# Dilated and plain sliding attention with a gated convolution: one score tile and one normalization per pair, constant matmuls at the start, evictions on ScalarE, plain v from DRAM, loads three groups ahead

## The chip, the cores and the metric

One core of a Trainium2 chip. The metric is the device time of one execution in microseconds (us). A run over 1.5% above the fastest of the same kernel counts as slow here; ratios use fast runs alone.

Engines: PE is TensorE (matmul and transpose), PEld its weight loads, DVE is VectorE, ACT is ScalarE, POOL is GpSimd, SP is the engine that issues most DMAs.

## The reference

```python
# q, k, v: (batch 8, heads 8, seq 576, dim 64)
scores = q @ k.T / sqrt(64)
mask_plain = (rel >= 0) & (rel < 32)                       # heads 0-3, rel = query - key
mask_dil   = (rel >= 0) & (rel < 128) & (rel % 4 == 0)     # heads 4-7
attn = softmax(where(mask, scores, -1e9));  x = attn @ v   # -> (8, 576, 512)
gate = sigmoid(causal depthwise conv of x, 5 taps)
out  = (gate * (x @ w_val)) @ w_out                        # fp32, (8, 576, 512)
```

The work is cut into 32 pairs of heads, four to a batch (two plain, two dilated). A pair is two halves: scores, exp, mask, product with v, normalization. Convolutions, value projections and output tiles of earlier pairs are put between these steps to keep PE busy. Two pairs of one kind in one batch form a group, which is the unit of loading.

## The kernel before

The order of instructions is written by hand and engines run their queues in order. The parts that matter:

```python
NET = 4
ets = [consts.tile([128, 2 * HB + 96], BF16, name=f"et{i}") for i in range(NET)]   # HB = 288
out_pool = tc.tile_pool(name="osb", bufs=4)
ps_sc = tc.tile_pool(name="ps_sc", bufs=2, space=PSUM)
...
def scores(i, hf):
    ps = ps_sc.tile([128, 2, 512], FP32, name="ps_sc")      # two banks, one for each head
    ...                                                     # 6 matmuls
    et = ets[(2 * i + hf) % NET]
    nc.scalar.activation(out=e3, in_=ps[:, :, 0:HB], func=AF.Exp, scale=scale)
...
def attn_v(i, hf):                                          # into the same tile, after the exp
    nc.tensor.matmul(out=ps[:, sl, n * AVS:n * AVS + D + 1], lhsT=et[...], rhs=rhs, ...)
def normalize(i, hf):                                       # reciprocal, then product, per half
...
for i in range(NP):
    if c % 2 == 0 and g + 2 < 2 * B:
        load_group(g + 2)
    ...                                  # casts of group g + 1, v casts, masks
    if i == 1:
        load_weights()                   # w_val and w_out, issued on POOL
    scores(i, 0); scores(i, 1)
    ...                                  # trans_x(i - 1)
    apply_mask(i, 0); pop_dense(0.5); pop_conv(i); apply_mask(i, 1)
    trans_main(g + 1, ...)               # transposes of the next group, evictions to ACT and DVE
    attn_v(i, 0); normalize(i, 0); pop_conv(i + 0.5)
    attn_v(i, 1); normalize(i, 1); pop_dense(1.5)
```

Names in the profile lines: `ps_sc` is the score tile in PSUM, `et` the exponentials, `xn` the normalized attention output, `xT` its transpose, `y_all` the gated value projections, `osb` an output tile in SBUF, `k_nat` and `k_b` the keys as loaded and as cast, and `qT`, `qA`, `kA`, `kB` the transposed queries and keys.

The softmax here doesn't subtract the row's maximum and nothing guards it: scores larger than these inputs give would overflow.

## Time and profile before

| | before |
|---|---|
| median of the runs, us | 208.59 (207.0 to 209.9) |
| start of pair 0, pair 4, pair 28, us | 11.36, 35.72, 167.19 |
| batches from pair 4 on, us | 21.79, 22.37, 22.57, 20.67, 22.50, 21.57 |
| busy: PE, DVE, ACT, POOL, us | 170.7, 136.3, 100.2, 51.6 |

A "batch" here is the time from the first score matmul of one pair to that of the fourth pair after it. The waits and busy times are in the prediction. The timeline of PE in the kernel before (start, length, line, operation; idle time before it in brackets), then that of ACT at the same place:

```profile
112.58 0.29 PE L357 MATMUL ps_sc<-qA,kA 64*128 64x128 bf16 x4
112.71 0.18 PE L357 MATMUL ps_sc<-qB,kB 64*128 64x32 bf16 x2
112.98 0.28 PE L357 MATMUL ps_sc<-qA,kA 64*128 64x128 bf16 x4
```

### The profile page before, as it was taken

How to read it: one execution, taken by the hardware profiler on the slowest of the kernel's cores; microseconds unless marked ns; L12 is line 12 of the kernel's file. 1: busy time of each engine (PE TensorE's matmuls, PEld its weight loads, DVE VectorE, ACT ScalarE, POOL GpSimd, SP SyncE). 2: the span in 40 equal slices, each digit the busy share in tenths (PEclk: the TensorE clock that was granted, in tenths of full speed). 3: DMA queues.
4: the chain of work that ended last, by engine and by line, in shares of the span. 5: the costliest groups of instructions: out<-in, count | busy, mean ns of one | idle time of the engine just before them, and what ended most of it. 6: DMA issues, size and time to landing. Idle time of an engine off the chain costs nothing.

```text
span 206.6 us, 5215 instructions
## 1 busy us (share of the span) xinstructions
PE 170.7 (83%) x2016; PEld 123.5 (60%) x2036; DVE 136.3 (66%) x370; ACT 100.2 (49%) x183; POOL 51.6 (25%) x99
## 2 busy tenths in 40 slices
PE   0277779879987999796979999779996998899990
PEld 0165556657655776565657766557675765675540
DVE  3357629589677966784679867758596856883510
ACT  2152442436644576354545755355743685354141
POOL 3063543026210450117011701062105303000000
PEclk9999999999999999999999999999999999999999
DMA  6968998399687985899489938995789766001435
GB/s 161 229 183 248 236 210 223 120 291 192 191 245 200 225 238 149 251 269 258 116 274 267 245 100 275 271 217 188 221 254 221 240 183 230 3 15 63 129 84 169
DMA packets 57186, 40.72 MB, mean 197 GB/s; under 512 B 25925, under 2 KB 52549, under 8 KB 57162
## 3 DMA queue, kind: packets, MB, share of 16 engines
q1 hardware_dynamic: 55280, 38.75, 72.6%
q0 software_dynamic: 1056, 1.05, 3.2%
q10 hardware_dynamic: 826, 0.60, 1.1%
q8 instruction: 16, 0.26, 0.6%
q14 instruction: 8, 0.07, 0.1%
HBM read 31.99 MB, written 9.44 MB: 201 GB/s over the span
## 4 chain that ended last, share of the span: by engine, by line
PE 39%; DMA 25%; DVE 14%; ACT 8%; SPq 6%; issue 4%; POOL 2%; ACTq 0%; POOLq 0%
DMA q_nat<-in_q_dram 22%; PE ps_moe L489 10%; PE ps_moe L459 10%; PE ps_moe L474 6%; DVE xn L408 5%; ACT et L360 3%; SPq L106 3%; PE ps_sc L389 3%; PE ps_sc L357 3%; PE ps_tr L286 3%; DMA vB_st<-in_v_dram 3%; ACT kA L307 2%; DVE y_all L480 2%; DVE et L373 2%; PE ps_tr L420 2%
## 5 line engine op out<-in xcount | busy, mean ns | idle before, releaser
L459 PE MATMUL ps_moe<-xT,conv_diag 128*128 128x288 bf16 (+1 forms) x384 | 53.1, 276 | 0.8 <-ACT osb L494 0.5
L360 ACT ACTIVATE et<-ps_sc 128x576 bf16<-128x576 f32 x64 | 38.6, 649 | 28.0 <-PE ps_sc L357 25.3
L474 PE MATMUL ps_moe<-xT,w_val_b 128*128 128x288 bf16 x256 | 39.9, 285 | 8.0 <-DVE y_all L480 7.3
L467 ACT ACTIVATE gate<-ps_moe 128x288 bf16<-128x288 f32 x64 | 26.7, 418 | 35.7 <-PE ps_moe L459 35.6
L459 PEld LDWEIGHTS <-conv_diag 128*128 128x128 bf16 x384 | 33.2, 101 | 8.7 <-issue 1.8
L408 DVE TENSOR_TENSOR xn<-ps_sc,rec 96x384 bf16<-96x384 f32 (+1 forms) x64 | 35.6, 555 | 2.2
L489 PE MATMUL ps_moe<-w_out_b,y_all 128*128 128x512 bf16 x124 | 33.9, 378 | 1.1
L480 DVE SCALAR_TENSOR_TENSOR y_all<-gate,ps_moe 128x288 bf16<-128x288 bf16 x64 | 27.6, 448 | 9.0 <-PE ps_moe L474 8.3
L474 PEld LDWEIGHTS <-w_val_b 128*128 128x128 bf16 x256 | 23.3, 97 | 17.1 <-issue 10.2
L494 ACT ACTIVATE osb<-ps_moe 128x512 f32<-128x512 f32 x36 | 21.5, 598 | 21.3 <-PE ps_moe L489 17.0
L435 DVE COPY xT<-ps_tr 128x576 bf16<-128x576 bf16 x32 | 14.6, 457 | 22.5 <-PE ps_tr L433 16.2
L171 POOL CAST vA<-v_st 128x512 bf16<-128x512 f32 x16 | 10.7, 671 | 56.0 <-DMA v_st<-in_v_dram 40.3
L389 PEld LDWEIGHTS <-et 128*128 128x128 bf16 x384 | 20.1, 102 | 6.0 <-DVE et L373 2.5
L489 PEld LDWEIGHTS <-y_all 128*128 128x128 bf16 x144 | 12.7, 97 | 11.8 <-issue 0.4
L403 DVE RECIPROCAL rec<-ps_sc 96x6 f32<-96x6 f32 (+1 forms) x64 | 11.9, 185 | 9.6 <-PE ps_sc L389 9.2
L373 DVE TENSOR_TENSOR et<-et,mask_p 128x576 bf16<-128x576 bf16 x32 | 15.2, 483 | 2.4 <-ACT et L360 1.9
L373 DVE TENSOR_TENSOR et<-et,mask_d 128x576 bf16<-128x576 bf16 x32 | 16.5, 532 | 0.2
L286 PE MATMUL ps_tr<-ident,k_b 128*128 128x128 bf16 x64 | 6.6, 242 | 11.2 <-POOL k_b L158 5.8
L168 POOL COPY vP<-vP 32x640 f32<-32x640 f32 x16 | 11.7, 752 | 16.6 <-DMA vP<-in_v_dram 13.9
L158 POOL CAST k_b<-k_nat 128x512 bf16<-128x512 f32 x14 | 9.0, 640 | 25.3 <-DMA k_nat<-in_k_dram 24.4
L301 ACT COPY kT<-ps_tr 128x1024 bf16<-128x1024 bf16 (+1 forms) x9 | 8.3, 917 | 13.0 <-PE ps_tr L286 12.9
L389 PE MATMUL ps_sc<-vP,et 128*128 128x65 bf16 x192 | 12.0, 200 | 2.3 <-DVE et L373 1.5
(66 smaller groups left out, 184.3 us busy)
## 6 DMA issues: line engine op xcount, KB each, us to landing
k_nat<-in_k_dram SPq DMA_DIRECT2D x15, 512.0 KB, 5.8
q_nat<-in_q_dram SPq DMA_DIRECT2D x15, 512.0 KB, 6.9
vP<-in_v_dram SPq DMA_DIRECT2D x8, 576.0 KB, 8.5
v_st<-in_v_dram SPq DMA_DIRECT2D x8, 512.0 KB, 4.2
vB_st<-in_v_dram SPq DMA_DIRECT2D x16, 128.0 KB, 5.0
out_dram<-osb SPq DMA_DIRECT2D x8, 256.0 KB, 3.5
out_dram<-osb SPq DMA_DIRECT2D x8, 224.0 KB, 3.1
out_dram<-osb SPq DMA_DIRECT2D x8, 192.0 KB, 3.4
```

Source lines behind the costliest of these rows:

```text
L286: nc.tensor.transpose(out=ps[:, z, TM * m:TM * m + TM], in_=src, identity=ident)
L360: nc.scalar.activation(out=e3, in_=ps[:, :, 0:HB], func=AF.Exp, scale=scale)
L373: nc.vector.tensor_tensor(out=e3, in0=e3, in1=m, op=ALU.mult)
L389: nc.tensor.matmul(out=ps[:, sl, n * AVS:n * AVS + D + 1], lhsT=et[:, sl * HB + col:sl * HB + col + 128], rhs=rhs, start=True, stop=True)
L408: nc.vector.tensor_tensor(out=dst, in0=av[:, :, :, 0:D], in1=rec[0:R, :, :, None].to_broadcast([R, 2, 3, D]), op=ALU.mult)
L435: nc.vector.tensor_copy(xTs[b % NXT][:, c, :, 2:], pr)
L459: nc.tensor.matmul(out=ps[:, o * T:(o + n) * T], lhsT=conv_diag[:, c, K - 1 - m, :], rhs=xt[:, c, r:r + n, off:off + T], start=(idx == 0), ...
L467: nc.scalar.activation(out=gate, in_=ps[:, 0:HB], func=AF.Tanh, scale=0.5)
L474: nc.tensor.matmul(out=ps[:, 0:HB], lhsT=w_val_b[:, mc, c * 128:(c + 1) * 128], rhs=xt[:, mc, 2 * G:2 * G + 2, 2:], start=(mc == 0), stop= ...
L480: nc.vector.scalar_tensor_tensor(out=y_all[:, c, b * S + G * HB:b * S + (G + 1) * HB], in0=gates.pop((b, c, G)), scalar=1.0, in1=ps[:, 0:H ...
L489: nc.tensor.matmul(out=ps, lhsT=y_all[:, c, 128 * n:128 * n + 128], rhs=w_out_b[:, c, :], start=(c == 0), stop=(c == NCH - 1),)
L494: nc.scalar.mul(out=osb, in_=ps, mul=0.5)
```

## The change

Its intent: warm PE early with matmuls on constants; halve the number of normalizations; take the 32 rows of overlap of plain v from DRAM instead of by POOL copies; move the qT, qA and kB evictions from DVE to ACT; give the loads one group more of a head start. Not in its short description, but in the diff: the next group's transposes move ahead of the masks, and the casts move two groups ahead, in front of the weight loads on POOL.

```diff
-    ps_sc = tc.tile_pool(name="ps_sc", bufs=2, space=PSUM)
+    ps_sc = tc.tile_pool(name="ps_sc", bufs=1, space=PSUM)
-    NET = 4
-    ets = [consts.tile([128, 2 * HB + 96], ...
+    NET = 2
+    ets = [consts.tile([128, 4 * HB + 96], ...
 ... (load of plain v as 128 overlapping rows; its POOL copies gone; masks rebuilt for the new layouts)
 def scores(i, hf):
-    ps = ps_sc.tile([128, 2, 512], FP32, name="ps_sc")
+    if hf == 0:
+        st[(i, "ps")] = ps_sc.tile([128, 4, 512], FP32, name="ps_sc")
+    ps = st[(i, "ps")][:, 2 * hf:2 * hf + 2, :]
 ...
 def attn_v(i, hf):
-    out=ps[:, sl, n * AVS:n * AVS + D + 1],
+    out=ps[:, 2 * hf, x * AVS:x * AVS + D + 1],
 ...
-def normalize(i, hf):      # reciprocal of 6, product of 384, per half
+def normalize(i):          # reciprocal of 12, product of 768, per pair
 ...
-    nc.vector.tensor_copy(t["qA"], ...)     # likewise qT, kB (kB in a new layout)
+    nc.scalar.copy(out=t["qA"], ...)
 ...
+    load_group(2)                            # at the start
+    warm(8)                                  # 128x512 matmuls on constants, 36 in all
 ... (in the loop over pairs)
-        load_group(g + 2)
+        load_group(g + 3)
 ... (casts of group g + 2 on POOL, ahead of load_weights)
         scores(i, 0)
         scores(i, 1)
+        trans_main(g + 1, ...)               # was behind apply_mask(i, 1)
         apply_mask(i, 0)
 ... (warm(2) or warm(3) at four places while i < 3)
         attn_v(i, 0)
-        normalize(i, 0)
         attn_v(i, 1)
-        normalize(i, 1)
+        normalize(i)
```

More of the change, by code (lines that the diff above doesn't have):

```diff
@@ L9 @@
 BF16 = mybir.dt.bfloat16
+I32 = mybir.dt.int32
 AF = mybir.ActivationFunctionType
@@ L68 @@
     ps_tr = ctx.enter_context(tc.tile_pool(name="ps_tr", bufs=2, space=PSUM))
-    ps_sc = ctx.enter_context(tc.tile_pool(name="ps_sc", bufs=2, space=PSUM))
+    ps_sc = ctx.enter_context(tc.tile_pool(name="ps_sc", bufs=1, space=PSUM))
     ps_moe = ctx.enter_context(tc.tile_pool(name="ps_moe", bufs=2, space=PSUM))
@@ L77 @@
     ident5 = consts.tile([8, 8], FP32, name="ident5")
-    mask_p = consts.tile([128, 4, 24], BF16, name="mask_p")
+    mask_p = consts.tile([128, NB, 96], BF16, name="mask_p")
+    junk = consts.tile([128, 512], BF16, name="junk")
+    same = consts.tile([128, 2], BF16, name="same")
+    par_i = consts.tile([128, 2], I32, name="par_i")
     mask_d = consts.tile([128, HB], BF16, name="mask_d")
@@ L81 @@
     kTs = [consts.tile([128, 2, KOFF + S], BF16, name=f"kT{i}") for i in range(NKT)]
-    NET = 4
-    ets = [consts.tile([128, 2 * HB + 96], BF16, name=f"et{i}") for i in range(NET)]
+    NET = 2
+    ets = [consts.tile([128, 4 * HB + 96], BF16, name=f"et{i}") for i in range(NET)]
     NVP = 2
@@ L130, in load_v @@
         if not dil:
+            dst = vPs[b % NVP].rearrange("p h n e -> p (h n) e")
+            first = 0
+            if b == 0:
+                nc.sync.dma_start(out=dst[32:128, 0, 0:D], in_=v[0, 0, 0:96, :])
+                first = 1
             nc.sync.dma_start(
-                out=vPs[b % NVP].rearrange("p h n e -> p (h n) e")[32:128, :, 0:D],
-                in_=v[b, 0:4].rearrange("h (t p) d -> p (h t) d", p=96))
+                out=dst[:, first:4 * NB, 0:D],
+                in_=bass.AP(
+                    tensor=v.tensor, offset=v.offset + (b * H * S + 96 * first - 32) * D,
+                    ap=[[D, 128], [96 * D, 4 * NB - first], [1, D]]))
         else:
@@ L139, in load_v @@
                 in_=v[b, 4:8, 0:RM, :].rearrange("h (p r) d -> p h (r d)", r=DIL))
-            for f in range(2):
-                nc.sync.dma_start(
-                    out=t["vBst"][64 * f:64 * f + 64].rearrange("p h j d -> p h (j d)"),
-                    in_=v[b, 4:8, DIL * TB:S, :].rearrange(
-                        "h (p f j) d -> f p h (j d)", f=2, j=2)[f])
+            nc.sync.dma_start(
+                out=t["vBst"].rearrange("p h j d -> p h (j d)"),
+                in_=v[b, 4:8, DIL * TB:S, :].rearrange("h (p j) d -> p h (j d)", j=2))
     def load_group(g):
@@ L165, in prep_v @@
         e = a + 2
-        if not dil:
-            vt = vPs[b % NVP]
-            nc.gpsimd.tensor_copy(
-                vt[0:32, a:e, 1:NB, 0:D], vt[96:128, a:e, 0:NB - 1, 0:D])
-        else:
+        if dil:
             nc.gpsimd.tensor_copy(
@@ L189 @@
     nc.scalar.dma_start(out=conv_nat, in_=moe_conv_w)
+    nc.vector.memset(junk, 1.0)
     nc.gpsimd.memset(ident, 0.0)
@@ L199 @@
     for et in ets:
-        nc.vector.memset(et[:, 2 * HB:], 1.0)
+        nc.vector.memset(et[:, 4 * HB:], 1.0)
     for i in range(NVP):
         nc.vector.memset(vPs[i][:, :, :, D:D + 1], 1.0 - 2.0 ** -9)
-        nc.vector.memset(vPs[i][0:32, :, 0, 0:D + 1], 0.0)
+        if i == 0:
+            nc.vector.memset(vPs[i][0:32, 0, 0, 0:D], 0.0)
     def band(dst, pattern, base):
@@ L222 @@
     )
-    band(mask_p, [[1, 4], [4, 24]], 32)
+    band(mask_p[:, 1, :].rearrange("p (r t) -> p r t", r=4), [[1, 4], [4, 24]], 32)
+    nc.gpsimd.tensor_copy(mask_p[:, 2:NB, :], mask_p[:, 1:2, :].to_broadcast([128, NB - 2, 96]))
+    nc.gpsimd.tensor_copy(mask_p[:, 0, :], mask_p[:, 1, :])
+    nc.gpsimd.memset(mask_p[0:32, 0, :], 0.0)
     for a in (0, 2):
@@ L248, in make_mask_d @@
         nc.gpsimd.tensor_copy(mask_d[:, TM:2 * TM], mask_d[:, 0:TM])
-        band(mask_d[:, 2 * TM:HB].rearrange("p (w t) -> p w t", w=2), [[64, 2], [1, TR]], TM - TB)
+        mb = mask_d[:, 2 * TM:HB].rearrange("p (w t) -> p w t", w=2)
+        nc.gpsimd.memset(mb, 1.0)
+        for (lo, up) in ((True, 0), (False, 0)):
+            sg = 1 if lo else -1
+            base = 2 * (TM - TB) if lo else 2 * (window - 1) - 2 * (TM - TB)
+            nc.gpsimd.affine_select(
+                out=mb, in_=mb, compare_op=ALU.is_ge, fill=0.0, base=base,
+                pattern=[[sg, 2], [2 * sg, TR]], channel_multiplier=-sg)
+        nc.gpsimd.iota(par_i, pattern=[[1, 2]], base=1, channel_multiplier=1)
+        nc.vector.tensor_scalar(
+            out=par_i, in0=par_i, scalar1=1, scalar2=None, op0=ALU.bitwise_and)
+        nc.vector.tensor_copy(same, par_i)
+        nc.vector.tensor_tensor(
+            out=mb, in0=mb, in1=same[:, :, None].to_broadcast([128, 2, TR]), op=ALU.mult)
     def setup_conv_w():
@@ L291, in trans_main @@
                     t["qT"] = qt_pool.tile([128, 2, DIL, T], BF16, name="qT")
-                nc.vector.tensor_copy(
-                    t["qT"][:, z0:z1, :, 0:TM],
-                    ps[:, z0:z1, :].rearrange("p z (r t) -> p z r t", r=DIL))
+                qd, qs = t["qT"][:, z0:z1, :, 0:TM], ps[:, z0:z1, :].rearrange("p z (r t) -> p z r t", r=DIL)
+                if g == 0:
+                    nc.vector.tensor_copy(qd, qs)
+                else:
+                    nc.scalar.copy(out=qd, in_=qs)
             else:
                 t["qA"] = qt_pool.tile([128, 2 * RM], BF16, name="qA")
-                nc.vector.tensor_copy(t["qA"], ps.rearrange("p z n -> p (z n)"))
+                nc.scalar.copy(out=t["qA"], in_=ps.rearrange("p z n -> p (z n)"))
         else:
@@ L305, in trans_main @@
                 t["kA"] = qt_pool.tile([128, 2 * RM], BF16, name="kA")
-                t["kB"] = qt_pool.tile([128, 8, 64], BF16, name="kB")
+                t["kB"] = qt_pool.tile([128, 4, 64, 2], BF16, name="kB")
                 nc.scalar.copy(out=t["kA"], in_=ps.rearrange("p z n -> p (z n)"))
-                nc.vector.tensor_copy(
-                    t["kB"][:, :, 0:TM - TB],
-                    ps.rearrange("p z (m t) -> p (z m) t", t=TM)[:, :, TB:TM])
+                nc.scalar.copy(
+                    out=t["kB"][:, :, 0:TM - TB, :],
+                    in_=ps.rearrange("p z (h w t) -> p (z h) t w", h=2, w=2)[:, :, TB:TM, :])
     def trans_rest(g):
@@ L327, in trans_rest @@
             nc.vector.tensor_copy(
-                t["kB"].rearrange("p (h w) t -> p h w t", w=2)[:, :, :, TM - TB:64],
-                pv[:, :, 0:64].rearrange("p w (h t) -> p h w t", h=4))
+                t["kB"][:, :, TM - TB:64, :],
+                pv[:, :, 0:64].rearrange("p w (h t) -> p h t w", h=4))
             nc.vector.tensor_copy(
@@ L352, in scores @@
                 else:
-                    x = 2 * (a + hf)
                     o = ps[:, sl, 2 * TM:HB]
-                    lhsT = t["kB"][p0:p0 + D, x:x + 2, :]
+                    lhsT = t["kB"][p0:p0 + D, a + hf, :, :]
                     rhs = t["qB"][p0:p0 + D, a + hf, :, :]
                 nc.tensor.matmul(out=o, lhsT=lhsT, rhs=rhs, start=True, stop=True)
-        et = ets[(2 * i + hf) % NET]
-        e3 = et[:, 0:2 * HB].rearrange("p (h n) -> p h n", h=2)
+        et = ets[i % NET]
+        e3 = et[:, 2 * hf * HB:2 * (hf + 1) * HB].rearrange("p (h n) -> p h n", h=2)
         nc.scalar.activation(out=e3, in_=ps[:, :, 0:HB], func=AF.Exp, scale=scale)
-        st[(i, "ps", hf)] = ps
-        st[(i, "et", hf)] = et
+        st[(i, "et")] = et
     def apply_mask(i, hf):
         b, c, dil, g, a = pair_info(i)
-        et = st[(i, "et", hf)]
-        if dil:
-            e3 = et[:, 0:2 * HB].rearrange("p (h n) -> p h n", h=2)
-            m = mask_d[:, None, :].to_broadcast([128, 2, HB])
-        else:
-            e3 = et[:, 0:2 * HB].rearrange("p (h n) -> p h n", h=6)
-            m = mask_p.rearrange("p r t -> p (r t)")[:, None, :].to_broadcast([128, 6, 96])
+        et = st[(i, "et")]
+        e3 = et[:, 2 * hf * HB:2 * (hf + 1) * HB].rearrange("p (h n) -> p h n", h=2)
+        m = mask_d if dil else mask_p[:, 3 * hf:3 * hf + 3, :].rearrange("p n q -> p (n q)")
+        m = m[:, None, :].to_broadcast([128, 2, HB])
         nc.vector.tensor_tensor(out=e3, in0=e3, in1=m, op=ALU.mult)
@@ L376, in attn_v @@
         b, c, dil, g, a = pair_info(i)
-        et, ps = st[(i, "et", hf)], st[(i, "ps", hf)]
+        et, ps = st[(i, "et")], st[(i, "ps")]
         for n in range(3):
@@ L388, in attn_v @@
                         rhs = vBs[b % NVD][:, a + hf, sl, 0:D + 1]
+                x = 3 * sl + n if dil else 2 * n + sl
                 nc.tensor.matmul(
-                    out=ps[:, sl, n * AVS:n * AVS + D + 1],
-                    lhsT=et[:, sl * HB + col:sl * HB + col + 128],
+                    out=ps[:, 2 * hf, x * AVS:x * AVS + D + 1],
+                    lhsT=et[:, (2 * hf + sl) * HB + col:(2 * hf + sl) * HB + col + 128],
                     rhs=rhs, start=True, stop=True)
-    def normalize(i, hf):
+    def normalize(i):
         b, c, dil, g, a = pair_info(i)
-        ps = st[(i, "ps", hf)]
         R = 128 if dil else 96
-        if hf == 0:
-            st[(i, "xn")] = xn_pool.tile([128, 2, 3, 2, D], BF16, name="xn")
-        xn = st[(i, "xn")]
-        av = ps[0:R, :, 0:3 * AVS].rearrange("p h (n e) -> p h n e", n=3)
-        rec = rec_pool.tile([128, 2, 3], FP32, name="rec")
+        xn = st[(i, "xn")] = xn_pool.tile([128, 2, 3, 2, D], BF16, name="xn")
+        av = st[(i, "ps")][0:R].rearrange("p (f s) c -> p f s c", f=2)[:, :, 0, 0:6 * AVS].rearrange(
+            "p f (x e) -> p f x e", x=6)
+        rec = rec_pool.tile([128, 2, 6], FP32, name="rec")
         nc.vector.reciprocal(out=rec[0:R], in_=av[:, :, :, D])
         if dil:
-            dst = xn[0:R, :, :, hf, :]
+            dst = xn[0:R].rearrange("p z n h d -> p h (z n) d")
         else:
-            dst = xn[0:R, hf, :, :, :].rearrange("p n h d -> p h n d")
+            dst = xn[0:R].rearrange("p z n h d -> p z (n h) d")
         nc.vector.tensor_tensor(
             out=dst, in0=av[:, :, :, 0:D],
-            in1=rec[0:R, :, :, None].to_broadcast([R, 2, 3, D]), op=ALU.mult)
+            in1=rec[0:R, :, :, None].to_broadcast([R, 2, 6, D]), op=ALU.mult)
     def trans_x(i):
@@ L546, in push_conv, with warm @@
             convs.append((t + 0.5 * G, ("c", b, c, G)))
+    def warm(n):
+        for _ in range(n):
+            ps = ps_moe.tile([128, 512], FP32, name="ps_moe")
+            nc.tensor.matmul(out=ps, lhsT=junk[:, 0:128], rhs=junk, start=True, stop=True)
+    warm(8)
     for z in range(2):
@@ L552 @@
             trans_rest(0)
+            warm(1)
+    setup_conv_w()
     for i in range(NP):
         b, c, dil, g, a = pair_info(i)
-        if c % 2 == 0 and g + 2 < 2 * B:
-            load_group(g + 2)
-        if a == 0 and g % 2 == 1 and g + 1 < 2 * B:
-            for z in (0, 2):
-                for name in ("k", "q"):
-                    cast(g + 1, name, z, nc.gpsimd)
+        if c % 2 == 0 and g + 3 < 2 * B:
+            load_group(g + 3)
         if i + 1 < NP:
@@ L565 @@
             make_perm()
+        g2 = g + 2
+        if g2 < 2 * B and g2 % 2 == 0:
+            cast(g2, "k" if a == 0 else "q", 0, nc.gpsimd)
+            cast(g2, "k" if a == 0 else "q", 2, nc.gpsimd)
         if i == 1:
@@ L569 @@
         scores(i, 1)
-        if i == 0:
-            setup_conv_w()
         if i > 0:
@@ L576 @@
                 queue_batch(b - 1)
-        if i < NCH:
-            make_conv_diag(i)
-        apply_mask(i, 0)
-        pop_dense(0.5)
-        pop_conv(i)
-        apply_mask(i, 1)
         if g + 1 < 2 * B:
@@ L588 @@
                 trans_rest(g + 1)
+        if i < NCH:
+            make_conv_diag(i)
+        apply_mask(i, 0)
+        if i < 3:
+            warm(2)
+        pop_dense(0.5)
+        pop_conv(i)
+        apply_mask(i, 1)
+        if i < 3:
+            warm(2)
         attn_v(i, 0)
-        normalize(i, 0)
         pop_conv(i + 0.5)
+        if i < 3:
+            warm(2)
         attn_v(i, 1)
-        normalize(i, 1)
+        normalize(i)
+        if i < 3:
+            warm(3)
         pop_dense(1.5)
```

## The prediction

> **What bounds the kernel now.** I read the engine totals first: TensorE (PE) busy 83%, VectorE (DVE) 66%, ScalarE (ACT) 49%, GpSimd (POOL) 25%. No engine is full on average, so the limit has to be found by stage. I took the start of each of the 32 pairs' score matmuls from the timeline of PE: pair 0 starts at 11.36 us, pair 4 (the second batch) at 35.72, pair 8 at 57.51, pair 28 at 167.19, and the end is 206.6. The busy times in just these stretches:
>
> ```profile
> 11.36:35.72 24.36, 18.98 (x185) 14.37 (x184) 16.15 (x37) 9.34 (x17) 12.41 (x24) 1.00 0.97 221
> ...
> 79.88:102.45 22.57, 19.53 (x251) 14.31 (x253) 15.84 (x43) 11.95 (x22) 5.65 (x10) 1.00 0.86 218
> 102.45:123.12 20.67, 19.31 (x251) 14.34 (x253) 16.53 (x43) 11.95 (x22) 6.10 (x10) 1.00 0.88 231
> 123.12:145.62 22.50, 19.47 (x250) 14.35 (x253) 15.74 (x43) 11.74 (x22) 5.75 (x10) 1.00 0.84 224
> ```
>
> The columns are length, then PE, weight loads, DVE, ACT and POOL busy. A batch in the steady state costs PE 19.3 to 19.5 us of 20.7 to 22.6: PE sets the pace and loses 1.4 us in the best batch and 3 in the others. What it loses them to is the list of PE's waits over the whole run:
>
> ```profile
> PE ps_moe L474 <- DVE y_all L480: 7.3, 7, 1.2
> PE ps_tr L286 <- POOL k_b L158: 5.8, 4, 1.7
> PE ps_tr L286 <- DVE k_b L158: 4.9, 1, 4.9
> PE ps_tr L317 <- DVE qT L292: 3.5, 1, 3.5
> PE ps_sc L357 <- DVE xn L408: 3.4, 9, 0.6
> ```
>
> The third and fourth belong to the first 10 us. The first comes once a batch: three value projections follow the last attention matmul, and the third waits for the `y_all` product that stands behind the normalization on DVE. The second is a DMA in disguise, since POOL's casts wait for loads:
>
> ```profile
> POOL k_b L158 <- DMA k_nat<-in_k_dram: 24.4, 6, 5.9
> POOL q_b L158 <- DMA q_nat<-in_q_dram: 9.1, 6, 1.8
> ```
>
> The chain of waits agrees: it spends 22% of the span in loads of q, at the start and again near 73, 86, 137 and 151 us. The first two batches are slow for another reason. The same convolution matmul, in the window from 34 to 36.5 us and in that from 36.5 to 45:
>
> ```profile
> L459 PE MATMUL ps_moe<-xT,conv_diag 128*128 128x288 bf16 x4 | 1.4, 443 | 0.0
> ```
>
> ```profile
> L459 PE MATMUL ps_moe<-xT,conv_diag 128*128 128x288 bf16 x9 | 1.9, 286 | 0.0
> ```
>
> A convolution of six matmuls takes 1.2 us from start to start before 36.5 us and 0.62 after it. PE runs at half its rate for the whole first batch and never again, although the granted clock reads 1.00 throughout.
>
> **What the Trainium skill says.** "TensorE: Matmul & The Clock Gate", Part 1, says that the array starts at half clock and that "activity releases the throttle", after about 3.4 us of sustained work, and that it falls back after an idle window. The trace agrees on the factor (443 against 286 ns), but not on the time: PE was 78% busy from 11.4 us on and needed 25 us. Part 4 of the page says that transposes do not count as activity in the same way, which would explain it. "DMA: Bandwidth & Descriptors", Specifications, asks for 512 B per descriptor for line rate. The trace agrees: from 46 to 49 us, where the 256 B packets of the plain v go, the queues move 188 GB/s, and in the best single microseconds of 1 KB packets about 340. "VectorE: DVE Perf Modes", The perf-mode tier table, gives a tensor-tensor product with any PSUM operand the 1x rate; the trace has 555 ns for 384 elements, about 1 ns an element beyond the fixed part, so merging two normalizations saves only fixed parts.
>
> **The change, part by part.**
>
> Constant matmuls: 36 of 128x512. Four such (one output tile) take about 0.86 us from start to start when warm, so 0.215 each, and 0.43 cold by the factor above. Eight stand before anything else, one in the preparation and 27 in pairs 0 to 2. That is 9 per pair: 1.9 us warm or 3.9 us cold. They fill idle time only partly. Pair 0 will stay cold, I estimate, because PE still idles until 9.5 us (the order on DVE still puts the second cast, which waits for k until 8.1 us, ahead of the eviction), and it costs up to 3 us there. From some 18 us on PE should be warm, so pairs 1 to 3 need about 5 us each against 5.7, 7.4 and 6.6 now. The weights are now issued on POOL after the casts of group 2, which wait for q at 25.5 us: about 26.5 us instead of 20.9. They took 11.0 and 14.4 us to land beside other loads; with less beside them I estimate w_val at 34 to 36 us, just when pair 4 first uses it (37.2 now). So the start gains about 1 us, not the 10 that the clock alone suggests.
>
> One normalization per pair: 64 reciprocals of 185 ns and 64 products of 555 ns become 32 and 32. A reciprocal of 12 is about 190 ns, a product of 768 about 555+384*0.98 = 930. DVE saves 11.9-6.1 + 35.6-29.8 = 11.6 us. But the score tile is now one of four banks, not two of two, so the next pair's scores wait for the whole normalization: 0.2 us completion, 0.2, 0.93, about 1.35 us after the last attention matmul. Where PE has two output tiles or two projections (1.0 to 1.7 us) in between, that is nearly hidden; where it has one output tile (0.86), 0.5 us shows. That is about one pair of the four.
>
> Evictions to ACT: qT 7 x 688, qA 8 x 686 and kB 8 x 358 ns leave DVE (13.2 us). On ACT they cost 1012 and 1032 as the k evictions do now, and kB about 475 by the two sizes of kT (586 for 512 elements, 1012 for 1024): 7.1+8.3+3.8 = 19.2 us. So DVE falls from 136 to about 111 us, ACT rises from 100 to 119, some 3.8 of 5.1 us a pair: neither bounds.
>
> Plain v from DRAM: 16 POOL copies of 752 ns go (11.7 us). The load grows from 96 to 128 rows: 8 x 768 = 6144 packets of 256 B more, 1.57 MB, 1.04 us of every batch at 188 GB/s. By the same rates a batch needs about 16.3 us of DMA now and 17.4 then, of 20.7: still below PE.
>
> Three groups ahead: a load gets one more group, about 10 us, before its use. The casts now stand two groups ahead too. This should take the 4.2 us of `k_b` waits after the first batch and the smaller losses around them.
>
> Sum for a steady batch: I laid the four pairs out by hand with start-to-start times from the timeline (scores 0.36, their transposes 0.45, projection 0.49, convolution 0.62, output tile 0.87, attention 0.2, exp 0.65, mask 0.45, xT 0.46). PE work is 19.0; the third projection still waits (0.8, was 1.16); the one pair with a short tail loses 0.5; the rest transposes now come right after the pair's other two and wait for a buffer (0.2 in two pairs). That gives 20.7 us against 21.9 on average from pair 4 to 28. I count five batches at -1.2, since the first has no output tiles and gains nothing: -6.0. Start -1.0. Tail -0.5 (one 0.96 us wait for a mask at 174 us). With +0.5 for the larger early v load: 208.6 - 7.0 = 201.6. I lean 1 us lower, since waits on loads also cost the drained matmul pipeline, which the idle column leaves out: 200.6.
>
> **Rivals.** (1) The serial chain through one score tile becomes the bound: scores 0.36, exp 1.2, masks 0.9, attention 0.4, normalization 1.35 and four handovers make about 4.6 us, against 4.75 us of PE work a pair. For it speaks that the longer ACT evictions sit in the same queues; against it, that conv and output work fills the gaps in the order that the build has. If each pair lost 0.3 us more, 28 pairs give +8: 208, no gain. (2) The start gets worse: cold fillers delay pairs 0 and 1 by 3 us, and late weights stop PE long enough to cool it again. Then +3 to +5: 204 to 206. (3) The warm-up works as meant: warm from about 5 us on, and pair 4 starts near 31 us. Against it stands the w_val landing. Then -3 more: 197, or 195 with no steady waits. (4) DMA becomes the bound: 17.4 of 20.7 us is 84%, and small loads hold the queue (the rate falls to about 92 GB/s in 119 to 124 us, once a batch). With a group in hand I give this little; it would make 204.
>
> **Range and chances.** The rivals spread from 195 to 208. I predict 200.5 us, with 194.5 to 206.5 for 8 in 10. Faster by over 2% means under 204.4: 0.75. Within 2%: 0.22. Slower by over 2% needs rivals 1 and 2 together: 0.03.
>
> **What would show it.** Convolution matmuls at 286 ns before 25 us: warm-up right. `k_b` and `k_nat` gone from PE's and POOL's waits after 40 us: the loads right. Waits of the scores for `xn` of about 0.5 us, once or twice a batch, and of the third projection for `y_all` of 0.8: the batch sum right. DVE near 111, ACT near 119 us: the evictions right. I am wrong if a batch still takes 21.9 us, if PE stops for w_val beyond 37 us, or if pair 4 starts before 32.

## More of the kernel before

```profile
112.93 1.19 ACT L360 ACTIVATE et<-ps_sc 128x576 bf16<-128x576 f32 x2 [1.00 <-DVE xn L408]
```

The second half's scores start 0.40 us after the first's, while the first exp (from 112.93) is already reading the first half's tile. The two halves are different tiles in different banks, and PE and ACT work side by side.

## The result, and the profile after

The changed kernel takes 248.97 us (248.14 to 250.58, four runs), the kernel before in the same rounds 209.25 (207.0 to 209.95). The ratio is 1.193, with a 95% interval of 1.181 to 1.205: 19% slower, where 200.5 us was predicted. A ratio here is the mean time of one kernel's fast runs over that of the other's fast runs of the same rounds, so not quite the ratio of the medians.

| | before | after |
|---|---|---|
| start of pair 0, pair 4, pair 28, us | 11.36, 35.72, 167.19 | 11.19, 42.46, 203.07 |
| last four batches before pair 28, us | 22.57, 20.67, 22.50, 21.57 | 25.95, 25.97, 26.22, 25.95 |

The time is lost everywhere. The start loses 7 us, the first two batches, which the table leaves out (28.98 and 27.54 us), 7 and 5, each of the four later ones 3 to 5, and the rest after pair 28 another 5. The same table of stretches as in the prediction (length, then PE, PEld, DVE, ACT, POOL), for one batch after:

```profile
98.98:124.93 25.95, 20.74 (x251) 14.93 (x253) 13.77 (x32) 14.90 (x25) 4.35 (x8) 1.00 0.71 193
```

PE has no more matmuls than before, the DMA share has fallen to 0.71, and all engines have room. This is a kernel that waits. The list of PE's waits over the whole run after (us in all, times, longest), to be held against the list in the prediction:

```profile
PE ps_sc L386 <- ACT et L389: 26.4, 32, 1.3
PE ps_sc L416 <- DVE et L398: 7.2, 16, 1.2
PE ps_moe L499 <- DVE y_all L505: 4.6, 7, 0.7
PE ps_sc L386 <- DVE xn L433: 4.2, 8, 1.4
```

The first line did not exist before: score matmuls waiting for an exp, once in each of the 32 pairs. The same place of a pair after, on PE and then on ACT:

```profile
131.55 0.30 PE L386 MATMUL ps_sc<-qT,kT 64*128 64x96 bf16 x6
132.60 0.30 PE L386 MATMUL ps_sc<-qT,kT 64*128 64x96 bf16 x6 [0.74 <-ACT et L389]
```

```profile
131.90 0.65 ACT L389 ACTIVATE et<-ps_sc 128x576 bf16<-128x576 f32 x1 [2.34 <-PE ps_sc L386]
132.94 0.65 ACT L389 ACTIVATE et<-ps_sc 128x576 bf16<-128x576 f32 x1 [0.39 <-PE ps_sc L386]
```

The second scores now start 1.05 us after the first, 0.05 us after the first exp has ended at 132.55; then the second exp waits 0.39 us for them. Nothing in the data asks for this: the second half writes two other banks. The built program shows where the wait comes from. In its list of PE's instructions with their semaphore waits, the first score matmul of a second half reads

```
L386 Matmult ps_sc_1468<-qT_1388,kT1_105 128x96 [waits Activation_49]
```

and it writes the same tile, `ps_sc_1468`, as the first half's scores. For this PSUM tile the framework orders a write after a read by whole tile: a write into banks 2 and 3 waits for the read of banks 0 and 1. All 32 second halves have such a wait on ScalarE in the built program; in the builds of e1 and e3, below, none has it. For the exp buffer in SBUF the same program orders by the columns touched: the weight loads of the first half's first five attention products wait for the first mask alone, that of the sixth for the second mask (see e3).

The parts that went as predicted are in the engine totals and groups. In the groups of ACT and of DVE (busy us, mean ns):

```profile
L325 ACT COPY qA<-ps_tr 128x1024 bf16<-128x1024 bf16 x8 | 8.1, 1012 | 1.3 <-PE ps_tr L312 1.3
L336 ACT COPY kB<-ps_tr 128x384 bf16<-128x384 bf16 x8 | 3.9, 485 | 0.0
```

```profile
L433 DVE TENSOR_TENSOR xn<-ps_sc,rec 128x768 bf16<-128x768 f32 x16 | 15.3, 958 | 0.6
L428 DVE RECIPROCAL rec<-ps_sc 128x12 f32<-128x12 f32 x16 | 3.7, 233 | 21.4 <-PE ps_sc L416 21.4
```

### The profile page after: what moved, and what is told of

Read it like the earlier page. It is cut to its first block, busy times and chain, and to the rows that moved or that the text cites. A ratio compares the mean times of both kernels' runs of the same rounds, so it can differ in the third digit from the quotient of the medians.

```text
span 247.9 us, 5248 instructions
## 1 busy us (share of the span) xinstructions
PE 190.5 (77%) x2050; PEld 129.7 (52%) x2072; DVE 118.3 (48%) x284; ACT 123.4 (50%) x206; POOL 38.6 (16%) x87
## 3 DMA queue, kind: packets, MB, share of 16 engines
q0 software_dynamic: 1056, 1.05, 2.7%
## 4 chain that ended last, share of the span: by engine, by line
PE 53%; DVE 22%; ACT 9%; DMA 6%; issue 5%; SPq 2%; ACTq 0%
PE ps_moe L484 12%; PE ps_moe L514 11%; ACT et L389 7%; PE ps_sc L386 6%; DVE xn L433 6%; PE ps_sc L416 6%; PE ps_moe L499 6%; DVE et L398 5%; DMA qk_rest<-in_k_dram 4%; DVE y_all L505 4%; PE ps_tr L312 3%; PE ps_moe L576 3%; DVE xT L460 3%; PE ps_tr L445 2%; DMA k_nat<-in_k_dram 2%
## 5 line engine op out<-in xcount | busy, mean ns | idle before, releaser
L389 ACT ACTIVATE et<-ps_sc 128x576 bf16<-128x576 f32 x64 | 41.6, 650 | 46.7 <-PE ps_sc L386 46.2
L484 PE MATMUL ps_moe<-xT,conv_diag 128*128 128x288 bf16 (+1 forms) x384 | 51.1, 269 | 1.3 <-DVE y_all L505 0.7
L514 PE MATMUL ps_moe<-w_out_b,y_all 128*128 128x512 bf16 x124 | 33.6, 379 | 1.1
L499 PEld LDWEIGHTS <-w_val_b 128*128 128x128 bf16 x256 | 24.2, 100 | 13.7 <-issue 6.6
L433 DVE TENSOR_TENSOR xn<-ps_sc,rec 96x768 bf16<-96x768 f32 (+1 forms) x32 | 30.6, 955 | 1.1
L416 PEld LDWEIGHTS <-et 128*128 128x128 bf16 x384 | 21.6, 99 | 17.7 <-DVE et L398 12.6
L428 DVE RECIPROCAL rec<-ps_sc 96x12 f32<-96x12 f32 (+1 forms) x32 | 7.4, 231 | 42.0 <-PE ps_sc L416 42.0
L386 PE MATMUL ps_sc<-qT,kT 64*128 64x96 bf16 x192 | 10.2, 212 | 15.8 <-ACT et L389 13.9
L386 PE MATMUL ps_sc<-qA,kA 64*128 64x128 bf16 x128 | 9.4, 224 | 14.8 <-ACT et L389 12.4
L386 PEld LDWEIGHTS <-kT 64*128 64x128 bf16 x192 | 5.9, 97 | 23.1 <-issue 19.5
L416 PE MATMUL ps_sc<-vP,et 128*128 128x65 bf16 x192 | 14.4, 200 | 4.1 <-DVE et L398 3.9
L386 PEld LDWEIGHTS <-kA 64*128 64x128 bf16 x128 | 5.4, 95 | 21.6 <-issue 16.5
L576 PE MATMUL ps_moe<-junk 128*128 128x512 bf16 x34 | 14.6, 534 | 2.0 <-DVE junk L196 1.5
```

What stands on the lines that cost most here:

```text
L386: nc.tensor.matmul(out=o, lhsT=lhsT, rhs=rhs, start=True, stop=True)
L416: nc.tensor.matmul(out=ps[:, 2 * hf, x * AVS:x * AVS + D + 1], lhsT=et[:, (2 * hf + sl) * HB + col:(2 * hf + sl) * HB + col + 128], rhs=rh ...
L433: nc.vector.tensor_tensor(out=dst, in0=av[:, :, :, 0:D], in1=rec[0:R, :, :, None].to_broadcast([R, 2, 6, D]), op=ALU.mult)
L484: nc.tensor.matmul(out=ps[:, o * T:(o + n) * T], lhsT=conv_diag[:, c, K - 1 - m, :], rhs=xt[:, c, r:r + n, off:off + T], start=(idx == 0), ...
L499: nc.tensor.matmul(out=ps[:, 0:HB], lhsT=w_val_b[:, mc, c * 128:(c + 1) * 128], rhs=xt[:, mc, 2 * G:2 * G + 2, 2:], start=(mc == 0), stop= ...
L514: nc.tensor.matmul(out=ps, lhsT=y_all[:, c, 128 * n:128 * n + 128], rhs=w_out_b[:, c, :], start=(c == 0), stop=(c == NCH - 1),)
```

## The experiments

Eighteen runs of seventeen kernels (e17 repeats e1) were made, all with correct results. They ran in five sets, each on one chip: e1 to e4, e5 to e8, e9 to e12, e13 to e16, e17 and e18. In these sets the kernel before had medians of 208.08, 206.04, 207.04, 208.09 and 208.73 us. Where kernels of different sets are compared, I use their ratios to the kernel before.

### Is it the merge? e1 to e4

**e1**: the changed kernel with the merge undone: two tiles of two banks, four exp buffers, a normalization per half; all else as changed. In short:

```diff
-ps_sc bufs=1, tile [128, 4, 512] per pair, NET = 2, normalize(i)
+ps_sc bufs=2, tile [128, 2, 512] per half, NET = 4, normalize(i, 0) and normalize(i, 1)
```

> The changed kernel with the one part undone that merged the two halves of a pair: two score tiles of two banks and two normalizations again, everything else as changed. Theory A (the merged tile is the cause: the second half's scores wait for the first half's exp, 26.4 us in the trace, and the next pair's scores for the whole normalization): a steady batch falls from 26.3 to under 22 us and the time from 249 to 203 to 212 us; the wait of the score matmuls for the exp is gone. Theory B (the evictions moved to ScalarE and ahead of the masks are the cause): it stays over 235 us. Theory C (the clock and the constant matmuls): 240 us or more, since the steady batch would not change.

Measured: 210.18 us (207.35 to 212.55), ratio 1.003 (0.992 to 1.014). 39 us come back.

**e2**: the reverse, the kernel before with the merge alone (the diff of e1 upside down, on the kernel before).

> The kernel before with only this part added: one score tile of four banks, one exp buffer and one normalization per pair. Theory A: 32 pairs lose about 0.9 us each, so 232 to 245 us, and the wait of the second half's scores for the exp appears with 20 to 28 us. Theory B and C: within 3% of 209 us.

Measured: 238.96 us (236.44 to 239.92), ratio 1.148 (1.139 to 1.157). Its waits of PE begin with the line that the changed kernel has, although nothing else of the change is in it:

```profile
PE ps_sc L359 <- ACT et L362: 25.9, 32, 1.0
PE ps_sc L359 <- DVE xn L408: 7.2, 10, 1.3
```

The merge alone makes the kernel slow, and without it the change is not slow.

**e3**: the changed kernel, with the scores of both halves issued ahead of both exps, so that no exp reads the tile before all its scores are written.

```diff
-scores(i, 0)  # 6 matmuls, exp
-scores(i, 1)  # 6 matmuls, exp
+scores(i, 0); scores(i, 1)  # 12 matmuls
+exps(i, 0); exps(i, 1)
```

> The changed kernel with both halves' score matmuls issued ahead of both exps, nothing else. In the build the wait of the second half's scores on ScalarE is gone, and the first exp waits for all twelve matmuls (0.18 us later) instead. Theory A: each pair's chain loses about 0.74 us of wait and gains 0.2, so some 0.55 x 32 = 17 us: 228 to 236 us; what remains over the kernel before is the scores' wait for the whole normalization. If the wait is only a symptom, hidden by other work that ends later, under 5 us: 244 to 249.

Measured: 218.41 us (215.49 to 220.72), ratio 1.042 (1.031 to 1.053). The wait for the exp is gone, and 30.6 us with it; I had expected 17. The wait was 26.4 us on PE alone, and, as I read it, it also delayed the second exp, and with it the mask, the attention products and the normalization behind it, for which the next pair waited again. What is left is the rest of the merge:

```profile
PE ps_sc L419 <- DVE et L401: 7.4, 19, 1.0
PE ps_sc L386 <- DVE xn L436: 5.5, 10, 1.4
```

The first is the shared exp buffer: the weight tile of the last attention matmul of a half is 128 columns wide and reaches into the other half's columns, so it waits for the second mask. The second is the wait that the prediction did name.

**e4**: the changed kernel without its 36 constant matmuls (`warm` and its calls removed).

> The changed kernel without the 36 constant matmuls. Pair 4 starts at 42.5 us in the changed kernel and at 35.7 in the kernel before. If the constants cost more than the clock gives back (14.6 us busy, and the clock falls back to half between 26 and 30 and between 42 and 48 us in the trace all the same): 242 to 247 us. If they help as meant: 251 to 256 us, with convolution matmuls at 444 ns for all of the first batch.

Measured: 246.18 us (245.58 to 248.13), ratio 1.187 (1.178 to 1.197). By the medians they cost 2.8 us in this kernel; by the ratios, whose intervals overlap, 1.2. In the profiles pair 4 starts at 38.73 us without them and at 42.46 with them. So they are a small part of the 40 at most.

### Where did the rest of the gain go? e5 to e8, e17

e1 has everything but the merge, and was predicted (in effect) at about 200, but took 210. Its first batches took 21.6 and 21.7 us, the third 27.6. ACT stood still twice, in the third and in the fifth. (The profile is of a slow run; e17 repeats it.) The line of ACT's waits, then ACT's and SP's timelines at the first place in e1:

```profile
ACT osb L518 <- DMA out_dram<-osb: 10.9, 2, 5.5
```

```profile
66.20 0.60 ACT L518 ACTIVATE osb<-ps_moe 128x512 f32<-128x512 f32 x1 [0.63 <-PE ps_moe L513]
...
82.28 0.60 ACT L518 ACTIVATE osb<-ps_moe 128x512 f32<-128x512 f32 x1 [5.45 <-DMA out_dram<-osb]
```

```profile
69.33 0.43 SPq L110 DMA_DIRECT2D k_nat<-in_k_dram  x1
...
72.59 3.01 SPq L127 DMA_DIRECT2D qk_rest<-in_q_dram  x4
...
76.73 1.19 SPq L524 DMA_DIRECT2D out_dram<-osb  x2
```

SP issues loads and stores from one queue in order. The output tile that ACT evicted at 66.20 us had its two stores issued only at 76.73, behind earlier stores and the twelve loads of a group, which hold SP from 69.3 to 76.6 (1.3 us of it a wait); each took 4.8 to 4.9 us more to land. ACT's fourth eviction after it, the one at 82.28, reuses its buffer and had to wait for them. ACT stopped, so did the exps behind it in its queue, and PE stood 5.4 us and ran cold after it (convolution matmuls of 128x288 at 429 to 448 ns; the granted clock is at half from 82.0 to 88.8 us).

**e5**: e1 with `osb` at `bufs=8` instead of 4.

> The changed kernel with two score tiles and two normalizations per pair (as in e1_halves), and 8 output buffers in SBUF instead of 4. Theory S: in e1 ScalarE stood 5.5 us twice because the output stores lay behind loads that are now issued three groups ahead on the same queue, and the four output buffers did not come free; with eight the two stalls go, PE stays warm, and the time is 196 to 202 us (210.2 less two times 5.5), with no wait of ACT for out_dram over 1 us. Theory D: the stores are only the place where a DMA shortage shows; the loads then come late instead and waits on k_nat or q_nat appear on POOL and PE: 206 to 211. Theory H: the two long batches are a hiccup of the profiled run and e1's 207 to 211 has other reasons: 206 to 211 with no DMA wait in the list.

Measured: 203.34 us (201.04 to 204.25), ratio 0.985 (0.977 to 0.993). The wait is not in the list any more, and the batches are 24.70, 21.43, 20.97, 20.91, 20.74 and 20.72 us. Theory S holds; the time is 1 us above its range, because of the first batch (see e9).

**e6**: e1 with 4 buffers, the loads two groups ahead and the casts one (as before).

> As e1_halves with its 4 output buffers, but loads issued two groups ahead and casts one group ahead, as in the kernel before. Theory S: the stores have fewer loads ahead of them, the stalls of 5.5 us go and the waits of PE for k_b come back (some 4 us in all): 199 to 205. If the order of the loads has nothing to do with the stalls: 207 to 212 with waits of ACT for out_dram of 5 us still there.

Measured: 206.86 us (205.97 to 207.82), ratio 1.006 (1.000 to 1.012). The stall is gone, and the waits of PE for `k_b` are back (5.6 us in three). The direction is that of theory S, the time is 2 us above its range. The head start of the loads is worth 3.5 us, but only with buffers for the stores.

**e7**: the kernel before with `bufs=8`.

> Control: the kernel before with 8 output buffers and nothing else. Before, ACT waited 1.5 us in all for stores, so theory S expects the same time within 1% (206 to 210). If it is over 2% faster, output buffers are a gain of their own and e5 tells less of the change.

Measured: 207.12 us (203.55 to 208.55) beside 206.04; no interval, since three of its four runs counted as slow. No gain is seen.

**e8**: e3 with `bufs=8`.

> The changed kernel with its merged tile and merged normalization, the scores of both halves ahead of both exps (as in e3_scores_then_exps), and 8 output buffers. e3's batches were all 22.4 to 23.8 us with no stall, so theory S expects nothing from the buffers here: 215 to 220; what stays over e5 is the wait for the whole normalization and for the second mask, 10 to 20 us. If it falls to 205 or less, the merged tile costs nothing beyond the order of scores and exps.

Measured: 217.07 us (215.66 to 217.79), ratio 1.055 (1.048 to 1.061). As expected: the buffers give it nothing, and one tile per pair still costs 13.7 us over e5 on the same chip, even with the scores ahead of the exps. PE's listed waits account for most of it: for masks 8.1 us against 3.1 in e5, for `xn` 4.8 against 0.6, for `y_all` 4.3 against 1.2.

**e17**: e1 unchanged, since its profile had fallen in the slow state.

> e1_halves once more, unchanged. If its stalls belong to the kernel (theory S): 205 to 211, ratio to before 0.99 to 1.01, at least one wait of ACT for out_dram of 4 us or more in the profile whatever its state. If they were a hiccup of the slow profile: no such wait and a ratio of 0.98 to 0.99, as e5_halves_8_out_buffers has.

Measured: 208.65 us (207.51 to 211.29), ratio 1.014 (1.004 to 1.024), the profile again of a slow run. The wait of ACT for `out_dram` stands at 10.9 us in two again (longest 6.9). No run of this kernel, ten in all, was under 207.35 us, while all four of e5 were under 204.3, so I take it that the fast runs have the stall too; a fast run's trace does not exist.

### The parts, once nothing stalls: e9 to e16, e18

In e5 the first batch after pair 4 took 24.7 us. PE stood for `w_val`, and then ran cold (twelve projection matmuls in 3.04 us; in e9 they take 1.85):

```profile
36.01 3.04 PE L498 MATMUL ps_moe<-xT,w_val_b 128*128 128x288 bf16 x12 [1.25 <-DMA w_val_b<-in_moe_w_val_dram]
```

**e9**: e5 with `load_weights()` at the start of pair 1, ahead of the casts that wait for q.

> e5 (two score tiles, two normalizations, 8 output buffers) with the two weight loads issued on POOL at the start of pair 1, ahead of v's casts and of the casts of group 2's q: about 22.4 us instead of 26.1. In e5 w_val landed at 36.0 us, PE stood 1.25 us for it in pair 4, then ran cold (444 ns instead of 285) for 3.5 us, and pairs 4 to 7 took 24.7 us where later batches took 20.7 to 21.4. If the late weights are the cause, the wait and the cold stretch go and the batch takes 21 to 21.5: 3 us less than e5, ratio to before 0.965 to 0.975. If only the cold clock has another cause, the gain is 1.2 us at most: ratio 0.98.

Measured: 201.95 us (200.66 to 203.14), ratio 0.977 (0.971 to 0.983). The wait and the cold stretch are gone and the batch takes 21.71 us, but pair 4 starts 1.6 us later than in e5 (34.50 against 32.88), so less is gained than I expected.

**e10**: e9 without the constant matmuls.

> e9 without the 36 constant matmuls. In the changed kernel they cost 2 to 3 us (e4), in a start that stalled for other reasons. With the stalls gone, theory W (they release the clock early and pay): PE stays cold until 25 us or later, pair 4 starts 2 to 4 us later than in e9, time 2 to 4 us more. Theory N (the fillers only take PE's time): the same or up to 2 us less than e9.

Measured: 200.32 us (200.0 to 202.82), ratio 0.974 (0.967 to 0.981): the same as e9 within the noise. The clock does what was meant with the constants (in e9 the clock is full from 17.3 us, and the first convolution matmuls, at 21.6, take 285 ns) and not without them (448 ns at 22 to 25 us in e10, 285 after 28). Yet pair 4 starts at 32.97 us without and at 34.50 with them. They buy their clock with as much time as it saves.

**e11**: e9 with one normalization per pair, but two tiles: both halves' attention products go into the two banks of the second half's tile.

```diff
-out=ps_of_half[hf][:, 0, ...]   ; normalize(i, 0), normalize(i, 1)
+out=ps_of_half[1][:, hf, ...]   ; normalize(i), over both banks
```

> e9 with one normalization per pair, but in two tiles of two banks: the attention products of both halves go into the two banks of the second half's tile, so that the next pair's first scores wait for nothing but the first exp, and only its second scores wait for the whole normalization. VectorE should save about 11 us of busy time. If the wait of the second scores for the first exp was the main fault of the merged tile, this is within 1% of e9. If the whole-pair normalization is itself too late (1.35 us after the last attention matmul against 0.9 for a half), the second scores wait 0.3 to 0.5 us in each pair and it is 5 to 12 us slower than e9.

Measured: 206.63 us (205.64 to 207.57), ratio 1.000 (0.995 to 1.005), 4.7 us over e9, though DVE's busy time fell from 129.0 to 120.0 us. Steady batches are 0.2 to 0.3 us longer than in e9; the batch after pair 4 is 24.09 with PE cold for a while again, after an idle time of 0.74 us. The waits listed for `xn` sum to 1.5 us only, so my account of a wait in each pair is not shown; the waits for `y_all` rise from 1.2 us to 3.7. What is shown is that DVE time saved here buys nothing.

**e12**: e9 with qT, qA and kB evicted by DVE.

> e9 with the qT, qA and kB evictions back on VectorE. VectorE's busy time rises by about 13 us to 140, ScalarE's falls by 19 to 97. The prediction held that neither engine bounds: within 1% of e9, with the third projection's wait for y_all growing from 0.2 to about 0.5 to 1 us a batch (up to 3 us more). If ScalarE's longer queue was costing more than that, it is faster than e9.

Measured: 217.60 us (216.82 to 219.16), ratio 1.054 (1.049 to 1.060): 15.6 us slower, where I and the prediction had held that neither engine bounds. PE's first wait, and a wait of DVE, in e12:

```profile
PE ps_sc L411 <- DVE et L393: 13.7, 10, 1.8
```

```profile
DVE kB L333 <- ACT kA L332: 13.0, 8, 3.2
```

DVE is hardly more loaded than in the kernel before (139.1 us against 136.3). But the evictions now stand ahead of the masks in its queue, and kB, in addition, waits there for ACT, which has two exps in front of kA.

**e14**: e12 with the next group's transposes behind the second mask, as before. **e15**: e9 with the same move. **e16**: e12 with the kB eviction alone on ACT.

```diff
 scores(i, 0); scores(i, 1)
-trans_main(g + 1, ...)
 apply_mask(i, 0); ...; apply_mask(i, 1)
+trans_main(g + 1, ...)        # e14 and e15
```

> e12 (evictions on VectorE) with the next group's transposes and their evictions back behind the second mask, where the kernel before has them. Theory O (order): on VectorE the evictions delayed the masks, so that putting them behind the masks takes back most of e12's loss: 202 to 208. Theory L (load: 139 us of VectorE busy is too much): it stays at 213 to 218.

> e9 (evictions on ScalarE) with the next group's transposes behind the second mask. Under theory O the place of the transposes is free when ScalarE evicts, or a little worse than e9 since the next pair's q and k come later: 201 to 206.

> e12 with the kB eviction alone on ScalarE; qT and qA stay on VectorE ahead of the masks. In e12 VectorE stood 13.0 us, 8 times 1.6, in front of kB until ScalarE had done kA. If that head-of-line wait is most of e12's loss: 203 to 207. If the qT and qA copies (0.69 us each) ahead of the masks matter as much: 208 to 213.

Measured: e14 201.77 us (201.35 to 203.80), ratio 0.976 (0.968 to 0.984); e15 199.48 (197.63 to 200.69), ratio 0.960 (0.950 to 0.970), better than I had expected; e16 205.14 (204.35 to 206.58), ratio 0.992 (0.983 to 1.001). So it is order, not load. With DVE evicting behind the masks the kernel is as fast as e9; ahead of them, kB's wait for ACT makes most of the loss (1.054 to 0.992) and the two longer copies the rest. Moving the transposes ahead of the masks, which the change did, was no gain on ACT either. Behind the masks ACT is a little better than DVE as the place for the evictions (e15 against e14: 2.3 us by the medians, but the intervals overlap).

**e13**: the changed kernel with its four-bank tile, but normalized in two halves.

> The changed kernel with its one tile of four banks per pair, but normalized in two halves, each right after its attention products. If the tile is at fault (theory A): the wait of the second scores for the first exp stays (26 us), and the second attention products now wait for the first normalization as well since they write the same tile: 245 to 270. If the merged normalization is at fault: 215 or less.

Measured: 251.46 us (250.06 to 254.54), ratio 1.212 (1.202 to 1.222). PE's waits begin

```profile
PE ps_sc L386 <- ACT et L389: 26.6, 32, 1.3
PE ps_sc L416 <- DVE et L398: 7.2, 16, 1.5
PE ps_sc L416 <- DVE xn L434: 6.9, 29, 0.3
```

The third is new: the second attention products wait for the first normalization, in another bank of the same tile. This parts the two: with the tile kept, undoing the merged normalization gives nothing back, so the tile costs the time. In two tiles the merged normalization goes with a loss of 4.7 us (e11). No run keeps the PSUM tile and gives each half its own exp buffer.

**e18**: e15 without the constant matmuls.

> e15 without the constant matmuls: two score tiles, 8 output buffers, weights early, transposes behind the masks, evictions on ScalarE. e10 against e9 gave nothing for the constants within the noise (0.974 against 0.977), so the ratio to before should be 0.955 to 0.965, as e15's 0.960, and the time 198 to 200 us; under 0.95 if the two add up, over 0.97 if the colder start shows once the later pairs are tighter.

Measured: 198.13 us (194.40 to 199.21) beside 208.73 (203.77 to 211.56). No interval: one run at 194.4 makes its other five count as slow. By the medians it is the fastest kernel; in the profile, which is of the run at 194.4, pair 4 starts at 30.60 us. Of the kernels that have an interval, e15 is the fastest; e5, e9, e10 and e14 lie clear of the kernel before too.

## Why the prediction was wrong

**The step that failed** is in the part on the normalization. It said that the score tile "is now one of four banks, not two of two, so the next pair's scores wait for the whole normalization", and put the loss at 0.5 us in "about one pair of the four". It looked for what the merge does between pairs and had no cost for the two halves within a pair, which use different banks. The wait inside the pair, of the second scores for the first exp, has no term in the sum. It measures 0.74 us and more in every pair, 26.4 us in all. e2 shows that it comes with the merge alone, e13 that it belongs to the tile, and e3 that issuing both scores first takes away 30.6 of the 40 us. I had read the order of the changed program's instructions, which is right as the prediction has it, but not the semaphore waits in that list, where the wait stands.

**The steady batch** shows the size of the missing term. Predicted 20.7 us, measured 25.95. In the batch from 98.98 us on, PE's listed waits are 3.3 us for the exp, 0.7 for `xn`, 0.6 for `y_all` and 0.3 for a mask. The predicted terms were 0.5 for `xn` and 0.8 for `y_all`: both near. The exp makes most of the rest. Each such wait also empties the matmul pipeline, which the idle column leaves out: in the kernel before most second halves start 0.15 us after the first, here 1.04, so 0.9 us later, where the column counts 0.74. The other 0.15 us is 0.6 a batch, an estimate. Over the whole run the profile of the changed kernel is 46.6 us longer than that of e5, which lacks the merge and the output stalls; of this 35.9 us are idle time of PE and 10.7 longer busy time, part of it at half clock.

**Rival 1** was the right family, a serial chain through one score tile, but at 0.3 us a pair. From 20.7 to 25.95 it is 1.3 us a pair. Its estimate of the chain, 4.6 us, counted the two scores as one block of 0.36 us. With the first exp, and its handovers, between them, the halves start 0.9 us further apart, so the chain would be about 5.5 us (an estimate), longer than PE's 4.75 us a pair. A steady pair took 6.5. That the chain is the bound is argued from this and not timed.

**The rest of the sum**, tested without the merge, came near. The steady batch of 20.7 us is what e5 has (20.72 to 21.43). Pair 4 was predicted at about 34.7 us and starts at 33.6 in e1, 32.9 in e5 and 34.5 in e9; in the changed kernel it starts at 42.5, as the wait is in pairs 0 to 3 too (with the merge alone, e2, at 41.2). The durations were right to 5% but for the reciprocal: qA 1012 ns (predicted 1032), kB 485 (475), the product of 768 elements 958 (930), the reciprocal of 12 elements 233 (190). One reading was low and had no part in the sum: the queues' best single microseconds move 375 to 384 GB/s in the kernel before, not 340. DVE fell to 118.3 us (predicted 111) and ACT rose to 123.4 (119). The waits for `k_b` are gone from PE's list.

**Where two terms were right and hid something.** The loads: the gain of about 4 us is there (e5 against e6: 3.5), but the earlier loads took the stores' place on SP, and four output buffers no longer sufficed (e1, e5, e17). In the changed kernel this stayed hidden (ACT has no wait for stores in its list), I take it because its slower batches leave the stores time. The evictions: "neither bounds" is true of the sums and not of the order (e12, e14, e16).

**The start.** The clock was released early as rival 3 has it (full from 18.1 us; the first convolution matmuls, at 23.7, take 287 ns), and fell back at 25 to 32 and 42 to 49 us in the changed kernel. The prediction's remark that the clock reads 1.00 throughout in the kernel before misreads the view: the trace's clock record begins only at 35.66 us, just where PE speeds up, and the view shows 1.00 where there is no record. Late weights stopping and cooling PE, which rival 2 feared, was seen in e5. But the constants bring nothing in e9 and e10, so the 1 us of gain at the start, if it comes, is not the clock's.

**What stays open**: why e11 loses 4.7 us to e9, of which its waits explain a part; the exact rule by which PE cools near pair 4 (it does in e5, e11, the changed kernel and others); and the trace of a fast run of e1. On the cooling the traces show more than single idle times. The granted clock falls at 36.07 us in e5, 36.02 in e11, and 24.92 and 41.99 in the changed kernel; in the 3.4 us before these, PE was busy for 1.59, 1.90, 1.74 and 1.44 us, where such stretches of the steady state in e5 have 2.7 to 3.4. But e15 kept its clock after a stretch with 1.48 us (from 23.17), so this is no rule either.

## What to carry to other kernels

Before merging two buffers into one tile, list every write and read of the tile between its birth and its release, and ask which of them the framework will now put in order, though they touch different parts; then look for these waits in the built program, where they can be read before anything runs. A busy total that falls is no gain by itself: here DVE lost 18 us of work and the kernel gained 40 us of time. When loads are issued earlier on the queue that also carries stores, give the stores more buffers.

## What the Trainium skill lacked or had wrong

- "Perfetto Trace Analysis", Matmuls, says that independent matmul groups should rotate through different PSUM banks, so that the eviction of one overlaps the next group's matmuls. It lacks that different banks are not enough: they had to be different tiles for the framework. Here the second scores wrote two other banks and still waited for the first exp, 26.4 us in 32 pairs; as two tiles (kernel before) they started 0.05 us after that exp had begun, as one tile 0.05 us after it had ended.
- "TensorE: Matmul & The Clock Gate", Part 1, says that the array falls back after at least one idle window of about 3.4 us. In e5 it was at half rate directly after an idle time of 1.25 us (twelve matmuls in 3.04 us against 1.85), with PE busy for 1.59 of the 3.42 us before, and after 1.41 us in the changed kernel; before both, PE had been doing short score matmuls, transposes or attention products. The advice of its section "Why this matters for your kernels", to keep TensorE busy for 4 us and more, is right for the clock (e9: 285 ns at 21.6 us, e10: 448 ns at 22 to 25) and bought no time (e9 and e10: ratios 0.977 and 0.974).
- "Perfetto Trace Analysis", DMA Optimizations, says that one issuing engine for inputs and another for outputs may make sense. It lacks what happens otherwise when loads are issued far ahead: here one group's loads held the stores behind them for 7.3 us, and ScalarE waited 10.9 us for output buffers in e1. No run tried two issuing engines.
- No page that I read tells that an eviction placed on another engine changes what stands behind it in that engine's queue: the same evictions on VectorE gave a ratio of 1.054 ahead of the masks (e12) and 0.976 behind them (e14).
